# Loading 128 partitions at once, a zero-padded product W, and unsplit float32 output matmuls for one half batch

## The chip, the cores and the metric

The kernel runs on one core of a Trainium2 chip. The metric is the device time of one launch in microseconds (us); a shorter time is better. Three runs of the kernel before gave 950.36, 950.41 and 951.36 us, median 950.41 us.

The core has a matmul engine (PE; its weight loads are the rows of PEld), a vector engine (DVE), an activation engine (ACT), a general engine (POOL) and a sync engine (SP), which here issues nearly all DMAs. Every engine works through its own instructions in order.

## The reference, cut to what matters

Three layers run one after the other. The first is a Nystrom attention over 4 batches, 8 heads, 576 tokens and a head dimension of 64 with 32 landmarks; the second and third are MLPs over the 2304 tokens with 512 features.

```python
q_lm = q.reshape(B, H, 32, 18, D).mean(axis=3)      # k_lm alike
A, Bm, C = sm(q, k_lm), sm(q_lm, k_lm), sm(q_lm, k)
for _ in range(6): Z = 2 * Z - Z @ Bm @ Z
x = (A @ Z @ C @ v)                                 # heads side by side: 2304 x 512
xn = x / sqrt(mean(x * x)) * rms_g
y = silu(xn @ w_gate) * (xn @ w_val) @ w_out        # d_ff 1536
out = (s * relu(y @ w_in2) ** 2 + b) @ w_out2       # d_ff 2048
```

The weights `w_gate`, `w_val`, `w_out`, `w_in2` and `w_out2` arrive as 8-byte floats and are turned into float32 on the chip.

## The kernel before, in words

**Attention and W.** For each batch, A (576 x 32 per head) is kept apart from W = Z C v (32 x 64 per head). The first MLP layer is (A W) w_gate; the kernel computes U = W w_gate first (`fused`), and then multiplies the normalised A with it (`first_mm`). The matrix `gw` holds W transposed and scaled by `rms_g`. One U is built for each of 4 batches x 12 column blocks f of 128 features (48 units, gate and value together). A head has 64 features, so U of one unit takes for each of two groups g four matmuls, one per head, with 64 rows of `gw` and 32 columns (L977).

**Loads.** The 128 partitions of `rawg` are two halves of 64, each with its own heads; the q and k loads (L438) and the loads of `w_gate` and `w_val` (L892) are therefore two DMAs of 64 partitions each. `narrow` loads a 128-column block of 8-byte weights into one of three `stage` buffers, ACT (L902, L904) and DVE (L906, L909) turn it into float32, and `stage` is free again after L906. Batch 0 decodes all blocks of the first MLP and stores the float32 result to DRAM (`keptg`, `kepto`); later batches read it back.

**Split matmuls.** For the big matmuls an operand is split into a high and a low part that the PE takes in one pass each (`split`: L867 or L868 for the high part, L869 for the low part), and three products of such parts stand for one float32 product (`PART3`). `first_mm` (L996), `out_mm` (L1036), `first_mm2` (L960) and `second_mm` (L1062) are such.

**Output matmuls of the first MLP.** A batch is worked on in two halves hf of 288 columns. `hidden` leaves silu(gate) x value of one f and hf in a slot of `hq_r` (a part of `hbuf` and later of `xbuf`); six units later `out_mm` multiplies it with a block of `w_out` (ring `rawo`, three slots) into four PSUM banks.

**Order.** A list scheduler (`Scheduler.run`) writes the order of all engines at build time, from a cost for each operation in microseconds and a key (due time), and it takes ring slots as its own clock says that they come free. Where it has the PE idle in the first 60 us of its clock it puts in small matmuls on ones (L1225) that keep the PE busy. A change of one cost moves instructions on all engines.

**Tail.** From 547 us on the second MLP runs alone (L960 and L1062); no line of it is touched.

Of the kernel before, what the change touches and what calls it, by code (L numbers as in the profile page):

```python
# [222 lines left out]
def t_dve(n):  # L223
    return 0.065 + 0.00104 * n
# [14 lines left out]
def t_mm(n):  # L239
    return 0.0004167 * (max(n, 200) + 32)  # L240
# [7 lines left out]
def tile_nystrom_attention_two_mlps(  # L248
# [39 lines left out]
    def ring(n, shape, name, dtype=F32):  # L288
        return Ring([Slot(sb.tile(shape, dtype, name=f"{name}{i}")) for i in range(n)], True)
# [20 lines left out]
    cm_r = ring(2, [128, 512], "cmag", I32)  # L310
    u_r = [ring(2, [128, 512], f"u{x}", F32R) for x in "hl"]
    w_r = [ring(2, [128, 512], f"w{x}", F32R) for x in "hl"]
    gw_r = ring(2, [128, 128], "gw")
    N_H = 9
    hbuf = sb.tile([128, 1536 + N_H * 288], F32, name="hbuf")
    th_r = Ring([Slot(hbuf[:, 512 * i:512 * i + 512]) for i in range(2)], True)
    h_r = Ring([Slot(hbuf[:, 1024:1536])], True)
# [47 lines left out]
    def consts(_):  # L365
# [10 lines left out]
        out=ident, in_=ones, pattern=[[-1, 128]], compare_op=ALU.is_equal,  # L376
        fill=0.0, base=0, channel_multiplier=1), r=["const"], w=["ident"])

    def load_small(e):
        for i in range(2):  # L380
            e.dma_start(out=gT[D * i:D * i + D], in_=rms_g.rearrange("(r k p) -> r p k", r=2, k=KD)[i])
        e.dma_start(out=s_sb, in_=s2.rearrange("(o k) -> o k", o=1).to_broadcast([128, 1]))
        e.dma_start(out=b_sb, in_=b2.rearrange("(o k) -> o k", o=1).to_broadcast([128, 1]))

# [11 lines left out]
    def attention(b, t0, t1):  # L396
# [38 lines left out]
        for nm, a in (("k", k), ("q", q)):  # L435
            for g in range(2):
                t = src[nm, g] = Buf(qk_r[nm, g])
                at(("sp", 4.1), -0.3 if b else 0, lambda e, t=t, a=a, g=g: [e.dma_start(  # L438
                    out=t.t[64 * i:64 * i + 64].rearrange("p (t d) -> p t d", d=D),
                    in_=a[b, 4 * i + 2 * g:4 * i + 2 * g + 2].rearrange("h (i t) d -> (h i) t d", t=SEG))  # L440
                    for i in range(2)], w=[t])
        vs = Buf(v_r)

        def vt():
            return vs.t.rearrange("p (j h d) -> p j h d", j=5, h=H)
# [213 lines left out]
        def c_side(g, p0):  # L659
# [52 lines left out]
            def cv_mm(_):  # L712
                for j in range(5):
                    n = min(128, S - 128 * j)
                    for h in range(4):
                        nc.tensor.matmul(
                            out=pV.t[32 * h:32 * h + 32, 0:D],
                            lhsT=eT.t[0:n, 128 * j + 32 * h:128 * j + 32 * h + 32],
                            rhs=vt()[0:n, j, 4 * (h // 2) + 2 * g + h % 2, :], start=(j == 0), stop=(j == 4))

            at(("pe", 1.3), p0 + 0.06, cv_mm, r=[(eT, 0), (eT, 1), vs], w=[pV, (Cv, "taken")])
            at({"dve": t_dve(64), "act": 0.1 + t_act(64)}, p0 + 0.07, lambda e: (
# [65 lines left out]
        def wt_mm(_):  # L788
            for g in range(2):
                for h in range(4):  # L790
                    p = slice(32 * h, 32 * h + 32)
                    nc.tensor.matmul(
                        out=pT[h % 2].t[D * (h // 2):D * (h // 2) + D, 32 * g:32 * g + 32],
                        lhsT=Cv.t[p, D * g:D * g + D], rhs=ZY.t[p, 64 * g:64 * g + 32], start=True, stop=True)

        at(("pe", 0.5), 0.62, wt_mm, r=[ZY, (Cv, 0), (Cv, 1)], w=[*pT, (gW, "taken")])
        for i in range(2):
            at(("dve", t_dve(64)), 0.62, lambda e, i=i: e.tensor_tensor(
                out=gW.t.rearrange("p (g c m) -> p g c m", g=2, c=2)[:, :, i],
                in0=pT[i].t[:, 0:64].rearrange("p (g m) -> p g m", g=2),  # L800
                in1=gT.rearrange("p (g c) -> p g c", g=2)[:, :, i:i + 1].to_broadcast([128, 2, 32]),
                op=ALU.mult), r=[pT[i], "small", (gW, "taken")], w=[(gW, i)])

        for hf in range(2):
            p0 = 0.7 + 0.15 * hf
# [64 lines left out]
            out=lo(), in0=src(), in1=hi().bitcast(F32), op=ALU.subtract), r=[*r, wh], w=[wl], pair=True)  # L870
        a.spare = b.spare = {"dve": spare}

    def by_head(x):

        return [x.rearrange("(r k p) f -> r p k f", r=2, k=KD)[i] for i in range(2)]

    def narrow(key, kind, f, part, dst, w, after=()):
        c = slice(128 * f, 128 * f + 128)
        wt = ((w_gate, w_val, w_out), (w_in2, None, w_out2))[kind - 1][part]
        st, a, m = Buf(st_r), Buf(ca_r), Buf(cm_r)  # L880

        def load(e):
            if part == 2:
                e.dma_start(out=st.t, in_=wt[c, :])
            else:
                to = st.t.rearrange("p (k f) -> p k f", k=KD)
                if kind == 2:
                    e.dma_start(out=to, in_=wt[:, c].rearrange("(k p) f -> p k f", p=128))
                    return
                for i in range(2):  # L890
                    p = slice(D * i, D * i + D)
                    e.dma_start(out=to[p], in_=by_head(wt[:, c])[i])  # L892

        def word(i):
            return st.t.bitcast(I32).rearrange("p (n t) -> p n t", t=2)[:, :, i]

        n_ops = len(S_.ops)
        op(("sp", 3.46), key - 12, load, w=[st])
        def low():
            return st.t.bitcast(U8).rearrange("p (n t) -> p n t", t=8)[:, :, 3]  # L900

        op(("act", 0.08 + t_act(512)), key, lambda e: e.activation(  # L902
            out=a.t, in_=word(1).bitcast(F32), func=ACTF.Copy, scale=2.0 ** -112), r=[st, "stage"], w=[a])
# [65 lines left out]
    def fused(key, b, f):  # L969
        r = first_weights(key - 10 if b == 0 else key - 6, b, f)  # L970
        pU, uh, ul = Buf(gv_r), Buf(u_r[0]), Buf(u_r[1])

        def mm(_):
            for g in range(2):
                for h in range(4):
                    k, p = 2 * g + h % 2, slice(D * (h // 2), D * (h // 2) + D)
                    nc.tensor.matmul(  # L977
                        out=pU.t[32 * h:32 * h + 32, 256 * g:256 * g + 256], lhsT=gw[b].t[p, 32 * k:32 * k + 32],
                        rhs=r.t[p, :, 128 * k:128 * k + 128], start=True, stop=True)

        op(("pe", U_PE), key, mm, r=[(gw[b], 0), (gw[b], 1), (r, 0), (r, 1)], w=[pU])
        op({"act": t_act(512), "dve": t_dve(512)}, key, lambda e: (
            e.activation(out=uh.t, in_=pU.t, func=ACTF.Copy) if e is nc.scalar
            else e.tensor_copy(out=uh.t, in_=pU.t)), r=[pU], w=[uh])
        op(("dve", t_dve(512)), key, lambda e: e.tensor_tensor(  # L985
            out=ul.t, in0=pU.t, in1=uh.t.bitcast(F32), op=ALU.subtract), r=[pU, uh], w=[ul])
        return uh, ul
# [35 lines left out]

    def out_mm(key, b, hf, f):
        r = out_weights(key - LEAD_O, b, hf, f)
        w = weights(key - LEAD_O, w_r, lambda: r.t, [r])
        h, hs = hid[b, hf, f], (Buf(hs_r[0]), Buf(hs_r[1]))
        split(key - 2, lambda: hs[0].t[:, 0:HC], lambda: hs[1].t[:, 0:HC], lambda: h.t, [h], *hs, HC)
        h_ops.extend(S_.ops[-2:])
        if f == 0:  # L1030
            acc1[b, hf] = [Buf(acc_r) for _ in range(KD)]
        A = acc1[b, hf]
        for c in range(KD):
            def mm(_, c=c):
                for i, (a, y) in enumerate(PART3):
                    nc.tensor.matmul(  # L1036
                        out=A[c].t[:, 0:HC], lhsT=w[a].t[:, 128 * c:128 * c + 128], rhs=hs[y].t[:, 0:HC],
                        start=(f == 0 and i == 0), stop=(f == F1 - 1 and i == 2))

            op(("pe", 3 * t_mm(HC)), key + 0.4 * c, mm, r=[*w, *hs], w=[A[c]])  # L1040
        if f < F1 - 1:
# [220 lines left out]
```

## Time and profile before

| what | value |
|---|---|
| median of 3 runs | 950.41 us |
| the profiled execution | 949.79 us |
| its span, first to last instruction | 948.1 us |
| PE busy | 894.3 us (94%) |
| DVE busy | 736.9 us (78%) |
| ACT busy | 447.7 us (47%) |
| DMA moved | 105.99 MB |
| mean granted PE clock | 0.986 |

The shares are means over stages that differ. Some 190 us pass before the PE runs without gaps: in this first stage all blocks of the first MLP are loaded and decoded, beside the attention of batches 0 and 1. From there to 547 us the first MLP runs with the attention of the later batches, and then the second MLP.

### The profile page before, as it was taken

To read this page: it belongs to the slowest core of one execution; us is meant where nothing else is said; L and a number is where in the kernel's file an instruction comes from. 1 tells how busy PE (TensorE), PEld (TensorE's weight loads), DVE (VectorE), ACT (ScalarE), POOL (GpSimd) and SP (SyncE) were. 2 spreads that over 40 slices of the span, in tenths; PEclk is the share of its full clock that TensorE was granted. 3 is DMA by queue.
4 is the path that set the end of the run, shared out by engine and by line. 5 is a ranking of instruction groups with operands and counts; after the bars stand their busy time and mean duration, and the time that the engine had idled before them with its cause. 6 is when DMAs were issued, how large, how long until landed. Compare 5 with 4: busy or idle time off the path is not lost.

```text
span 948.1 us, 17201 instructions
## 1 busy us (share of the span) xinstructions
PE 894.3 (94%) x6523; PEld 740.1 (78%) x6523; DVE 736.9 (78%) x1473; ACT 447.7 (47%) x898; POOL 127.9 (13%) x158
## 2 busy tenths in 40 slices
PE   7888988699998999999998999999999999999998
PEld 4566765589877988788887978888888888888886
DVE  6877888998888888879999976676667666666686
ACT  4555465453555344656767333343334333433354
POOL 0460035331363012300000000000000000000000
PEclk9999999799999999999999999999999999999999
DMA  8989878685344432337887200010001000100010
GB/s 174 236 204 274 220 221 243 210 291 160 100 119 131 137 108 84 101 123 246 278 269 241 89 1 1 0 37 9 1 1 45 0 1 1 45 1 0 13 34 22
DMA packets 72787, 105.99 MB, mean 112 GB/s; under 512 B 25856, under 2 KB 46336, under 8 KB 72704
## 3 DMA queue, kind: packets, MB, share of 16 engines
q1 hardware_dynamic: 72512, 104.62, 38.5%
q8 instruction: 51, 0.84, 0.4%
q14 instruction: 32, 0.26, 0.1%
q10 hardware_dynamic: 192, 0.26, 0.1%
HBM read 90.70 MB, written 14.16 MB: 111 GB/s over the span
## 4 chain that ended last, share of the span: by engine, by line
PE 72%; DVE 15%; DMA 6%; issue 4%; ACT 2%; SPq 1%; DVEq 0%; ACTq 0%
PE bank L1062 21%; PE bank L960 20%; PE bank L996 11%; PE bank L1036 10%; PE bank L977 3%; DVE cmag L906 3%; DVE wl L869 2%; DMA stage<-in_moe_w_val_dram 2%; DMA stage<-in_moe_w_out_dram 1%; DMA stage<-in_moe_w_gate_dram 1%; PE bank L1225 1%; PE bank L638 1%; DVE bank L840 1%; DVE hbuf L1013 1%; DVE ul L985 1%
## 5 line engine op out<-in xcount | busy, mean ns | idle before, releaser
L996 PE MATMUL bank<-xh,uh 128*128 128x288 f32 x384 | 124.0, 323 | 17.6 <-DVE ul L985 11.0
L1036 PE MATMUL bank<-hh,wh 128*128 128x288 f32 x384 | 118.8, 309 | 4.9 <-DVE wh L868 3.9
L960 PE MATMUL bank<-xh,uh 128*128 128x512 f32 (+1 forms) x320 | 119.1, 372 | 1.0 <-ACT hbuf L1203 1.0
L960 PE MATMUL bank<-xh,ul 128*128 128x512 f32 (+1 forms) x320 | 118.6, 371 | 0.0
L960 PE MATMUL bank<-xl,uh 128*128 128x512 f32 (+1 forms) x320 | 117.4, 367 | 0.0
L1203 ACT ACTIVATE hbuf<-bank 128x512 f32<-128x512 f32 (+1 forms) x79 | 44.0, 556 | 152.3 <-PE bank L960 152.2
L1036 PE MATMUL bank<-hl,wh 128*128 128x288 f32 x384 | 115.0, 299 | 0.8 <-DVE hl L869 0.7
L1036 PE MATMUL bank<-hh,wl 128*128 128x288 f32 x384 | 114.5, 298 | 0.7 <-DVE wl L869 0.7
L1062 PE MATMUL bank<-wh,hh 128*128 128x512 f32 x288 | 114.3, 397 | 0.3 <-DVE hh L868 0.3
L996 PE MATMUL bank<-xh,ul 128*128 128x288 f32 x384 | 114.4, 298 | 0.0
L996 PE MATMUL bank<-xl,uh 128*128 128x288 f32 x384 | 114.3, 298 | 0.0
L1062 PE MATMUL bank<-wl,hh 128*128 128x512 f32 x288 | 113.8, 395 | 0.0
L1062 PE MATMUL bank<-wh,hl 128*128 128x512 f32 x288 | 113.6, 394 | 0.0
L996 PEld LDWEIGHTS bank<-xh,uh 128*128 128x128 f32 x384 | 72.8, 190 | 43.1 <-DVE ul L985 15.4
L1036 PEld LDWEIGHTS bank<-hh,wh 128*128 128x128 f32 x384 | 73.3, 191 | 11.4 <-DVE wh L868 4.4
L869 DVE TENSOR_TENSOR hl<-hbuf,hh 128x512 fp32r<-128x512 f32 (+2 forms) x137 | 77.4, 565 | 3.0 <-ACT hh L867 0.5
L869 DVE TENSOR_TENSOR wl<-rawo,wh 128x512 fp32r<-128x512 f32 x94 | 70.7, 754 | 5.5 <-ACT wh L867 1.3
L1036 PEld LDWEIGHTS bank<-hl,wh 128*128 128x128 f32 x384 | 73.3, 191 | 2.0 <-DVE hl L869 1.5
L1036 PEld LDWEIGHTS bank<-hh,wl 128*128 128x128 f32 x384 | 73.1, 190 | 1.3 <-DVE wl L869 1.2
L996 PEld LDWEIGHTS bank<-xl,uh 128*128 128x128 f32 x384 | 73.3, 191 | 0.1
L996 PEld LDWEIGHTS bank<-xh,ul 128*128 128x128 f32 x384 | 73.4, 191 | 0.0
L868 DVE CAST uh<-region 128x512 fp32r<-128x512 f32 x57 | 24.3, 427 | 58.8 <-PE bank L960 58.8
(181 smaller groups left out, 1811.4 us busy)
## 6 DMA issues: line engine op xcount, KB each, us to landing
rawo<-kepto SPq DMA_DIRECT2D x84, 256.0 KB, 3.1
rawg<-keptg SPq DMA_DIRECT2D x36, 512.0 KB, 3.9
stage<-in_moe_w_out_dram SPq DMA_DIRECT2D x28, 512.0 KB, 5.0
stage<-in_moe_w_in_dram SPq DMA_DIRECT2D x16, 512.0 KB, 5.4
stage<-in_moe_w_gate_dram SPq DMA_DIRECT2D x24, 256.0 KB, 5.7
stage<-in_moe_w_val_dram SPq DMA_DIRECT2D x24, 256.0 KB, 5.5
keptg<-rawg SPq DMA_DIRECT2D x12, 512.0 KB, 6.9
region<-in_k_dram SPq DMA_DIRECT2D x16, 288.0 KB, 5.6
```

Source lines behind the costliest of these rows:

```text
L638: nc.tensor.matmul(out=ps.t[:, 0:HC], lhsT=part(u, "bd")[:, 128 * e:128 * e + 128], rhs=part(y, "t").rearrange("p (t e i) -> p t e i", e=2 ...
L840: e.reciprocal(out=pS.t[:, 0:HC], in_=pS.t[:, 0:HC])
L868: else e.tensor_copy(out=hi(), in_=src())), r=r, w=[wh], pair=True)
L869: b = op({"dve": t_dve(n), "pool": t_pool(n)}, key, lambda e: e.tensor_tensor(out=lo(), in0=src(), in1=hi().bitcast(F32), op=ALU.subtract) ...
L906: op(("dve", t_dve(512)), key, lambda e: e.scalar_tensor_tensor(out=m.t, in0=word(1), scalar=-2 ** 31, in1=m.t, op0=ALU.bitwise_and, op1=A ...
L960: nc.tensor.matmul(out=ps.t[:, 0:n], lhsT=w[a].t[:, ks], rhs=x[y].t[:, kd, 0:n], start=(kd == 0 and i == 0), stop=(kd == KD - 1 and i == 2))
L977: nc.tensor.matmul(out=pU.t[32 * h:32 * h + 32, 256 * g:256 * g + 256], lhsT=gw[b].t[p, 32 * k:32 * k + 32], rhs=r.t[p, :, 128 * k:128 * k ...
L985: op(("dve", t_dve(512)), key, lambda e: e.tensor_tensor(out=ul.t, in0=pU.t, in1=uh.t.bitcast(F32), op=ALU.subtract), r=[pU, uh], w=[ul])
L996: nc.tensor.matmul(out=ps.t[:, 0:HC], lhsT=u[a].t[:, 256 * g + 128 * part:256 * g + 128 * part + 128], rhs=x[y].t.rearrange("p k n -> p (k ...
L1036: nc.tensor.matmul(out=A[c].t[:, 0:HC], lhsT=w[a].t[:, 128 * c:128 * c + 128], rhs=hs[y].t[:, 0:HC], start=(f == 0 and i == 0), stop=(f == ...
L1062: nc.tensor.matmul(out=A[c].t, lhsT=hs[a].t[:, s], rhs=w[y].t, start=(f == 0 and i == 0), stop=(f == F2 - 1 and i == 2))
L1203: e.activation(out=r.t[:, 0:n], in_=ps.t[:, 0:n], func=ACTF.Relu) if e is nc.scalar
```

## The change

q and k are loaded with four heads in a row on 128 partitions, one DMA instead of two; `w_gate` and `w_val` come as feature = 128 k + partition, one DMA of 512 KB instead of two of 256 KB. A chunk of 128 features holds two heads, so `gw` gets 256 columns instead of 128: for each chunk a block of 128 x 64 with the two heads on its diagonal and zeros elsewhere. POOL writes the zeros once at the start; DVE fills the diagonal in four operations of 64 partitions instead of two of 128. U takes four matmuls of 128 rows and 64 columns instead of eight of 64 rows and 32 columns.

For batch 0, hf 0 (12 of the 96 steps of `out_mm`), one float32 matmul on `rawo` and the hidden slot takes the place of three on split parts, so that no split is made of either. The hidden ring loses one slot (`N_H` 9 to 8).

```diff
-    gw_r = ring(2, [128, 128], "gw")
-    N_H = 9
+    gw_r = ring(2, [128, 256], "gw")
+    N_H = 8
...
+    def gw_zero(e):
+        for s in gw_r.slots:
+            e.memset(s.t, 0.0)
+    op(("pool", 0.6), -30, gw_zero, w=["gw0"])
...
-                at(("sp", 4.1), -0.3 if b else 0, lambda e, t=t, a=a, g=g: [e.dma_start(
-                    out=t.t[64 * i:64 * i + 64].rearrange("p (t d) -> p t d", d=D),
-                    in_=a[b, 4 * i + 2 * g:4 * i + 2 * g + 2].rearrange("h (i t) d -> (h i) t d", t=SEG))
-                    for i in range(2)], w=[t])
+                at(("sp", 3.64), -0.3 if b else 0, lambda e, t=t, a=a, g=g: e.dma_start(
+                    out=t.t.rearrange("p (t d) -> p t d", d=D),
+                    in_=a[b, 4 * g:4 * g + 4].rearrange("h (i t) d -> (h i) t d", t=SEG)), w=[t])
...
-                for i in range(2):
-                    p = slice(D * i, D * i + D)
-                    e.dma_start(out=to[p], in_=by_head(wt[:, c])[i])
+                e.dma_start(out=st.t.rearrange("p (k f) -> p k f", k=KD),
+                            in_=wt[:, c].rearrange("(k p) f -> p k f", p=128))
...
-                        out=pU.t[32 * h:32 * h + 32, 256 * g:256 * g + 256], lhsT=gw[b].t[p, 32 * k:32 * k + 32],
-                        rhs=r.t[p, :, 128 * k:128 * k + 128], start=True, stop=True)
+                        out=pU.t[64 * i:64 * i + 64, 256 * g:256 * g + 256], lhsT=gw[b].t[:, 64 * k:64 * k + 64],
+                        rhs=r.t[:, :, 128 * k:128 * k + 128], start=True, stop=True)
...
+        h, whole = hid[b, hf, f], (b, hf) == (0, 0)
+        if whole:
+            w, hs = [r], [h]
+        else:
+            w = weights(key - LEAD_O, w_r, lambda: r.t, [r])
+            hs = (Buf(hs_r[0]), Buf(hs_r[1]))
+            split(key - 2, lambda: hs[0].t[:, 0:HC], lambda: hs[1].t[:, 0:HC], lambda: h.t, [h], *hs, HC)
...
+                if whole:
+                    nc.tensor.matmul(out=A[c].t[:, 0:HC], lhsT=r.t[:, 128 * c:128 * c + 128], rhs=h.t,
+                                     start=(f == 0), stop=(f == F1 - 1))
+                    return
...
-            op(("pe", 3 * t_mm(HC)), key + 0.4 * c, mm, r=[*w, *hs], w=[A[c]])
+            op(("pe", 0.49 if whole else 3 * t_mm(HC)), key + 0.4 * c, mm, r=[*w, *hs], w=[A[c]])
```

The scheduler writes a new order. On SP, which issues the loads, this stands before after the small loads of the beginning; `in_v` is the v of batch 1 in 18 DMAs, the numbers behind `stage` are its three slots:

```order
L438 DMA region<-in_k_dram 64x1152 x4
L438 DMA region<-in_q_dram 64x1152 x4
L892 DMA stage_90<-in_moe_w_val_dram 64x4x128 x2
L892 DMA stage_91<-in_moe_w_gate_dram 64x4x128 x2
L922 DMA keptg_113<-rawg_84 128x1024
L892 DMA stage_92<-in_moe_w_val_dram 64x4x128 x2
L450 DMA region<-in_v_dram 32x8x64 x18
L892 DMA stage_90<-in_moe_w_gate_dram 64x4x128 x2
```

And in the changed kernel, at the same place on SP:

```order
L443 DMA region<-in_k_dram 128x1152 x2
L443 DMA region<-in_q_dram 128x1152 x2
L454 DMA region<-in_v_dram 32x8x64 x18
L886 DMA stage_90<-in_moe_w_val_dram 128x4x128
L886 DMA stage_91<-in_moe_w_gate_dram 128x4x128
L886 DMA stage_92<-in_moe_w_val_dram 128x4x128
L917 DMA keptg_113<-rawg_84 128x1024
L886 DMA stage_90<-in_moe_w_gate_dram 128x4x128
```

The 18 loads of v have moved ahead of three weight loads (the value block of unit 0 and both blocks of unit 1).

On DVE, around the decode of the second block of `w_out` (`rawo_88`), this stands before:

```order
L906 SCALAR_TENSOR_TENSOR cmag_96<-stage_92,cmag_96 128x512
L909 SCALAR_TENSOR_TENSOR rawo_88<-ca_94,cmag_96 128x512
L868 CAST wh_102<-rawo_88 128x512
L985 TENSOR_TENSOR ul_99<-bank_67,uh_97 128x512
L869 TENSOR_TENSOR wl_104<-rawo_88,wh_102 128x512
L1013 SCALAR_TENSOR_TENSOR hbuf<-hbuf,bank_68 128x288
```

And in the changed kernel:

```order
L901 SCALAR_TENSOR_TENSOR cmag_95<-stage_92,cmag_95 128x512
L904 SCALAR_TENSOR_TENSOR rawo_88<-ca_93,cmag_95 128x512
L980 TENSOR_TENSOR ul_99<-bank_68,uh_97 128x512
L1008 SCALAR_TENSOR_TENSOR hbuf<-hbuf,bank_67 128x288
L625 SCALAR_TENSOR_TENSOR region<-region,bank_69 128x128
L901 SCALAR_TENSOR_TENSOR cmag_96<-stage_90,cmag_96 128x512
```

The two split operations of `rawo_88` are gone, and the next decode follows sooner. Over the whole program DVE has 11 fewer low parts of `w_out` (L869), 7 fewer high parts (L868) and 6 fewer low parts of hidden blocks than before, ACT 14 fewer high parts, POOL 7 fewer low parts.

## Rows read from the trace of the kernel before

**Rows 1.** Windows by stage: stretch, length, engine busy us (instructions), PE clock, DMA share, GB/s.

```profile
50.00:97.00 47.00, 41.58 (x351) 32.54 (x351) 34.97 (x64) 27.43 (x55) 13.89 (x19) 0.93 0.96 248
97.00:190.00 93.00, 73.63 (x731) 56.59 (x730) 81.84 (x175) 49.27 (x107) 26.95 (x32) 0.91 0.78 220
190.00:350.00 160.00, 156.22 (x1482) 137.34 (x1481) 136.97 (x304) 75.24 (x162) 51.33 (x64) 1.00 0.49 152
...
547.00:948.00 401.00, 395.80 (x1800) 325.04 (x1800) 267.79 (x481) 153.16 (x272) 0.00 (x0) 1.00 0.05 13
```

**Rows 2.** Chain of waits, 0 to 190 us: start, length in us, what.

```profile
3.97 7.01 DMA region<-in_q_dram
...
36.03 7.33 DMA stage<-in_moe_w_val_dram
...
67.42 5.18 DMA stage<-in_moe_w_gate_dram
...
76.65 6.95 DMA stage<-in_moe_w_val_dram
...
96.53 6.76 DMA stage<-in_moe_w_gate_dram
...
113.89 0.44 DVE wh L868
114.35 0.69 DVE wl L869
...
177.35 5.47 DMA region<-in_k_dram
...
188.29 0.69 DVE wl L869
```

**Rows 3.** DMA issues on the page: tile, queue, count, KB each, us to landing.

```profile
stage<-in_moe_w_in_dram SPq DMA_DIRECT2D x16, 512.0 KB, 5.4
stage<-in_moe_w_gate_dram SPq DMA_DIRECT2D x24, 256.0 KB, 5.7
```

**Rows 4.** Windows, three short stretches, columns as in rows 1.

```profile
4.00:10.00 6.00, 4.43 (x33) 3.24 (x32) 3.60 (x2) 2.40 (x6) 0.00 (x0) 1.00 1.03 229
62.00:92.00 30.00, 24.86 (x225) 19.71 (x225) 23.39 (x46) 16.36 (x34) 6.36 (x9) 0.94 1.04 274
196.00:208.00 12.00, 12.00 (x107) 10.48 (x106) 11.48 (x21) 6.80 (x14) 6.77 (x9) 1.00 0.97 317
```

**Rows 5.** Timelines of PE (first row) and of the SP queue: start, us, what.

```profile
28.91 0.90 PE L716 MATMUL bank<-region 128*32 128x64 f32 x40
...
42.63 11.96 SPq L450 DMA_DIRECT2D region<-in_v_dram  x18
54.69 1.26 SPq L892 DMA_DIRECT2D stage<-in_moe_w_gate_dram  x2
```

**Rows 6.** Groups by line, 97 to 190 us: busy us, mean ns, idle before.

```profile
L869 DVE TENSOR_TENSOR wl<-rawo,wh 128x512 fp32r<-128x512 f32 x12 | 10.3, 854 | 0.4
...
L868 DVE CAST wh<-rawo 128x512 fp32r<-128x512 f32 x9 | 4.2, 472 | 0.4
...
L869 DVE TENSOR_TENSOR hl<-hbuf,hh 128x288 fp32r<-128x288 f32 x6 | 2.7, 444 | 0.0
```

**Rows 7.** Chain of waits just behind 190 us, columns as in rows 2.

```profile
194.68 1.60 PE bank L1036 x12
196.28 1.00 PE bank L977 x16
```

**Rows 8.** Timeline of PE: two float32 matmuls of 128x128 by 288, back to back.

```profile
41.55 0.65 PE L835 MATMUL bank<-region,ones 128*128 128x288 f32 x2
42.04 0.65 PE L835 MATMUL bank<-xbuf,ones 128*128 128x288 f32 x2
```

**Rows 9.** Windows of 40 ns, line L488 alone: PE and PEld busy (records in flight).

```profile
11.54:11.58 0.04, 0.02 (x2) 0.02 (x2) 1.00 0.84 230
...
11.70:11.74 0.04, 0.04 (x4) 0.04 (x2) 1.00 1.41 346
```

More of the change, by code (lines that the diff above doesn't have):

```diff
@@ L377, in tile_nystrom_attention_two_mlps @@
         fill=0.0, base=0, channel_multiplier=1), r=["const"], w=["ident"])
+    def gw_zero(e):
+        for s in gw_r.slots:
+            e.memset(s.t, 0.0)
+    op(("pool", 0.6), -30, gw_zero, w=["gw0"])
     def load_small(e):
-        for i in range(2):
-            e.dma_start(out=gT[D * i:D * i + D], in_=rms_g.rearrange("(r k p) -> r p k", r=2, k=KD)[i])
+        e.dma_start(out=gT, in_=rms_g.rearrange("(k p) -> p k", p=128))
         e.dma_start(out=s_sb, in_=s2.rearrange("(o k) -> o k", o=1).to_broadcast([128, 1]))
@@ L718, in cv_mm @@
                             lhsT=eT.t[0:n, 128 * j + 32 * h:128 * j + 32 * h + 32],
-                            rhs=vt()[0:n, j, 4 * (h // 2) + 2 * g + h % 2, :], start=(j == 0), stop=(j == 4))
+                            rhs=vt()[0:n, j, 4 * g + h, :], start=(j == 0), stop=(j == 4))
             at(("pe", 1.3), p0 + 0.06, cv_mm, r=[(eT, 0), (eT, 1), vs], w=[pV, (Cv, "taken")])
@@ L792, in wt_mm @@
                     nc.tensor.matmul(
-                        out=pT[h % 2].t[D * (h // 2):D * (h // 2) + D, 32 * g:32 * g + 32],
+                        out=pT[h // 2].t[D * (h % 2):D * (h % 2) + D, 32 * g:32 * g + 32],
                         lhsT=Cv.t[p, D * g:D * g + D], rhs=ZY.t[p, 64 * g:64 * g + 32], start=True, stop=True)
         at(("pe", 0.5), 0.62, wt_mm, r=[ZY, (Cv, 0), (Cv, 1)], w=[*pT, (gW, "taken")])
[L797 to L802, printed above, removed]
+        for i, j in ((0, 0), (0, 1), (1, 0), (1, 1)):
+            at(("dve", t_dve(64)), 0.62, lambda e, i=i, j=j: e.tensor_tensor(
+                out=gW.t.rearrange("p (g c m) -> p g c m", g=2, c=2)[64 * j:64 * j + 64, :, i, 32 * j:32 * j + 32],
+                in0=pT[i].t[64 * j:64 * j + 64, 0:64].rearrange("p (g m) -> p g m", g=2),
+                in1=gT.rearrange("p (g c) -> p g c", g=2)[64 * j:64 * j + 64, :, i:i + 1].to_broadcast([64, 2, 32]),
+                op=ALU.mult), r=[pT[i], "small", "gw0", (gW, "taken")], w=[(gW, i, j)])
         for hf in range(2):
@@ L871, in split @@
         a.spare = b.spare = {"dve": spare}
-    def by_head(x):
-        return [x.rearrange("(r k p) f -> r p k f", r=2, k=KD)[i] for i in range(2)]
     def narrow(key, kind, f, part, dst, w, after=()):
@@ L885, in load @@
             else:
[L886 to L890, printed above, removed]
-                    p = slice(D * i, D * i + D)
-                    e.dma_start(out=to[p], in_=by_head(wt[:, c])[i])
+                e.dma_start(out=st.t.rearrange("p (k f) -> p k f", k=KD),
+                            in_=wt[:, c].rearrange("(k p) f -> p k f", p=128))
         def word(i):
@@ L974, in mm @@
             for g in range(2):
-                for h in range(4):
-                    k, p = 2 * g + h % 2, slice(D * (h // 2), D * (h // 2) + D)
+                for i in range(2):
+                    k = 2 * g + i
                     nc.tensor.matmul(
-                        out=pU.t[32 * h:32 * h + 32, 256 * g:256 * g + 256], lhsT=gw[b].t[p, 32 * k:32 * k + 32],
-                        rhs=r.t[p, :, 128 * k:128 * k + 128], start=True, stop=True)
-        op(("pe", U_PE), key, mm, r=[(gw[b], 0), (gw[b], 1), (r, 0), (r, 1)], w=[pU])
+                        out=pU.t[64 * i:64 * i + 64, 256 * g:256 * g + 256], lhsT=gw[b].t[:, 64 * k:64 * k + 64],
+                        rhs=r.t[:, :, 128 * k:128 * k + 128], start=True, stop=True)
+        op(("pe", U_PE), key, mm, r=[*[(gw[b], i, j) for i in range(2) for j in range(2)], (r, 0), (r, 1)], w=[pU])
         op({"act": t_act(512), "dve": t_dve(512)}, key, lambda e: (
@@ L1025, in out_mm @@
         r = out_weights(key - LEAD_O, b, hf, f)
[L1026 to L1029, printed above, removed]
+        h, whole = hid[b, hf, f], (b, hf) == (0, 0)
[5 more added lines that the diff above has]
+            split(key - 2, lambda: hs[0].t[:, 0:HC], lambda: hs[1].t[:, 0:HC], lambda: h.t, [h], *hs, HC)
+            h_ops.extend(S_.ops[-2:])
         if f == 0:
```

## The prediction

> **What bounds the kernel now.** I read the windows by stage first. In the last 401 us the PE is busy for 395.8 us and the DMA for 5% [rows 1]; nothing of the change stands there. From 190 to 350 us the PE is busy for 156.2 of 160 us, so that stretch is paid by PE work. The slack lies ahead of 190 us: from 97 to 190 us the PE is busy for 73.6 of 93 us at a granted clock of 0.91, DVE for 81.8 us (88%), the DMA for 78%; from 50 to 97 us the DMA for 96% and the PE for 41.6 of 47 us, fillers among them. No engine alone bounds this first stage; the chain of waits says who ends last, and it goes back and forth between landing weights and DVE. The reader is to see there five landings of 64-partition loads behind the attention's first one, at 5.2 to 7.3 us each, and between them the split and decode operations of DVE [rows 2]. So the change is priced in the first 190 us, and what the stage loses in length the total loses, as all behind it follows in order on a PE that is full.
>
> **The loads.** A 64-partition load moves slowly: from 4 to 10 us, when the q and k halves are nearly all there is, the DMA engines are busy all the time (1.03) at 229 GB/s; from 62 to 92 us, where weight halves are mixed with 128-partition stores, at 274/1.04 = 263 GB/s; from 196 to 208 us, with 128-partition transfers alone but a few, at 317/0.97 = 327 GB/s [rows 4]. The changed q, k, gate and value loads have the shape of the last kind; `w_in` has exactly the new shape (512 KB, 1 KB pieces) and lands in 5.4 us, while one half of a gate block, 256 KB, takes 5.7 us [rows 3] and is issued as the second of two that take 1.26 us together [rows 5]. On the chain stand four gate or value landings: 7.33, 5.18, 6.95 and 6.76 us, in all 26.2 us, each with the first half's issue of some 0.63 us ahead of it: 28.7 us. At 5.4 us each they are 21.6 us: 7.1 us less. The k load at 177 us loses one issue of two and about as much landing, 1 us. The opening q landing at 11.0 us comes earlier: 8 loads of 295 KB are 2.36 MB, at 327 instead of 229 GB/s 3.1 us less; DVE's reductions follow it, so I take 1.5 us (ends 0 and 3.1). Sum of the loads 9.6 us; ends 1.5 (issues alone) and 15.
>
> [...]
>
> **The moved v.** The 18 v loads hold SP for 11.96 us, and the next gate load goes out only at 54.69 us [rows 5]. In the new order they stand ahead of three weight loads instead of behind them. The buffer is in use by batch 0 until the matmuls of L716 end, at 29.8 us now [rows 5]; if v starts at 28 to 30 us, the value block of unit 0 goes out near 41 us instead of the 35 to 36 us of now (its landing starts at 36.03 us [rows 2]), while the gate block of unit 2, now held to 54.69 us, is free of the block. Ends: 5 us lost, if unit 0's first matmuls wait for that value block; 6 us won, half the block. I take 0.
>
> **DVE.** Gone are 11 low parts of `w_out` at 0.854 us, 7 high parts at 0.472 and 6 low hidden parts at 0.444 [rows 6]: 9.4 + 3.3 + 2.7 = 15.4 us, all in the 12 steps of batch 0's first half, which lie in this stage. DVE's added operations on `gw` are a few of some 0.2 us per batch, 0.4 us. On the chain I count five low parts between 114.35 and 188.29 us, 4.4 us, five high parts of 0.44 us, 2.2 us, and two hidden parts, 0.7 us (the first and the last stand in [rows 2]): 7.3 us that certainly ended last. ACT and POOL lose work too, but neither is bound here. Ends: 3.5 us, if the next path is close behind, and 15.
>
> **PE.** An unsplit float32 matmul of this shape follows its predecessor after 0.49 us [rows 8]; four make 1.96 us. Now 12 passes take 1.60 us [rows 7]. So each of 12 steps costs 0.36 us more, 4.3 us in all. The PE is idle for 93 - 73.6 = 19.4 us of the second window [rows 1]; I take a quarter on the chain, 1.1 us lost. Ends 0 and 4.3.
>
> **U.** Sixteen records now take 1.00 us [rows 7], four at a time. The new U has 8 records of 128 rows and 64 columns. The landmark matmuls (L488) have just that form, and their records start in pairs: two in flight at 11.54, four at 11.70 us [rows 9]. A record of 256 columns takes 0.49/2 x 256/288 = 0.218 us; four pairs make 0.87 us, about as now. I cost it at 0. Ends: 0.1 us won per unit (48 units, 5 us), or, one after the other, 8 x 0.218 = 1.74 us, 0.74 us lost per unit.
>
> [...]
>
> **Sum.** 9.6 + 0 + 7.3 - 1.1 + 0 = 15.8 us off the chain of the first stage. Three resources are close together there, so other paths will end soon after the one that was cut; I keep three quarters, 11.9 us. 949.79 - 11.9 = 937.9 us for an execution like the profiled one; the median of the runs lies 0.6 us above it: 938.5 us.
>
> **The rivals.**
> - *More: the stage falls to what DVE needs.* From 50 to 190 us DVE is busy for 35.0 + 81.8 = 116.8 us; less 15 it is 101.8. Just behind the stage DVE runs at 11.48/12 = 96% [rows 4]; at that rate the 140 us become 106, floor 916 us. Halfway between the forecast and this floor: 927 us. For it: DVE is at 88% already. Against: the order is fixed at build time and each engine waits in it.
> - *Less: the loads gain nothing but an issue.* If HBM or latency sets the landings, 1.5 + 7.3 - 1.1, three quarters of it, is 5.8 us: 944.6 us.
> - *No change:* the cover is complete, and landings that stay late take back what DVE gives: 949 to 951 us.
> - *Slower: the buffers are held by the PE.* Before, a `rawo` slot and a hidden slot came free when DVE had split them; now only when the PE's fourth matmul has run. With three `rawo` slots the decode of step n + 3 waits for the PE's step n, and DVE works in order: behind a blocked decode queue the low parts of U and the hidden products, for which the PE waits. If each of 9 decodes costs one step's PE time, 9 x 1.96 = 17.6 us are added to the forecast: 956 us. It decides once a decode is blocked for more than 1.3 us on the mean (11.9/9). Against it: a step's three-slot lead is one and a half units.
> - *Slower: U's records run one after the other.* 0.74 us x 36 units behind the first stage, where the PE is full, is 27 us: 965 us. Rows 9 speak against it.
>
> **How the numbers follow.** Forecast 938.5 us: 0.53 (its own range 931 to 945). More, 927: 0.15. Less, 945: 0.13. No change: 0.06. Buffers, 956: 0.10. U, 965: 0.03. A difference of 0.2%, 1.9 us, is about what a measurement can tell from no change. Faster: 0.53 + 0.15 + 0.13 = 0.81. Same 0.06. Slower 0.13. The range from 924 to 951 us leaves out most of the last two cases and the far tail of the second.
>
> **What would show it.** Right: gate and value landings near 5.4 us or less on single issues of 512 KB; the DMA above 290 GB/s when busy between 60 and 95 us; a PE without gaps from some 178 us instead of 190; the tail still 401 us; U's 8 records in about 1 us. Wrong: DVE waits ahead of the `rawo` decodes that PE ends (buffers); U near 1.7 us; landings that stay at 6 to 7 us (less); a stage end at or behind 190 us.

## The result, and the profile after

The changed kernel takes 922.54 us (median of 4 runs, 920.90 to 924.32); the kernel before took 950.38 us beside it (947.47 to 951.36). The ratio is 0.9712 with a 95% interval of [0.9683, 0.9742]: 27.8 us less, where 11.9 were forecast. Four more executions on another chip gave a median of 922.98 us and a ratio of 0.9695 [0.9665, 0.9725]. The direction was right; the time lies just below the range.

The profiled execution took 924.32 us with a span of 922.3. First the windows by stage of the changed kernel, columns as in [rows 1], with the two stretches of [rows 4] that its loads fill, and one of 10 us (147 to 157) in which the PE still loses time:

```profile
4.00:10.00 6.00, 5.68 (x40) 4.32 (x39) 5.37 (x3) 3.61 (x9) 0.00 (x0) 1.00 1.10 347
62.00:92.00 30.00, 25.66 (x208) 19.10 (x206) 25.15 (x51) 19.42 (x44) 5.12 (x6) 1.00 0.82 268
50.00:97.00 47.00, 41.98 (x326) 31.77 (x325) 36.92 (x78) 27.95 (x59) 10.73 (x13) 0.96 0.77 251
97.00:190.00 93.00, 89.07 (x753) 68.49 (x753) 80.94 (x160) 56.46 (x114) 34.76 (x42) 0.96 0.82 269
147.00:157.00 10.00, 6.41 (x35) 5.66 (x34) 9.15 (x16) 9.88 (x15) 1.14 (x2) 0.66 0.72 222
190.00:350.00 160.00, 155.12 (x1432) 135.32 (x1430) 134.04 (x312) 75.66 (x163) 40.57 (x51) 1.00 0.42 127
547.00:922.00 375.00, 370.81 (x1724) 309.96 (x1722) 254.83 (x458) 146.26 (x260) 0.00 (x0) 1.00 0.05 13
```

From 97 to 190 us the PE is now busy for 89.07 of 93 us instead of 73.63, at a clock of 0.96 instead of 0.91 [rows 1]. In the opening the DMA moves 347 GB/s instead of 229, and from 62 to 92 us 268/0.82 = 327 GB/s while busy instead of 263 [rows 4].

The chain of waits of the changed kernel, 0 to 190 us (start, length in us, what), answers to [rows 2]:

```profile
2.20 8.48 DMA region<-in_q_dram
...
41.33 4.89 DMA stage<-in_moe_w_val_dram
...
49.94 4.65 PE bank L1228 x23
...
67.95 5.65 DMA stage<-in_moe_w_val_dram
...
79.22 6.43 DMA stage<-in_moe_w_gate_dram
...
133.75 4.17 DMA stage<-in_moe_w_val_dram
...
149.99 0.61 DVE ul L980
150.65 1.81 PE bank L991 x6
...
158.92 1.01 PE bank L972 x8
...
160.92 1.94 PE bank L1035 x8
```

The gate and value landings are still there, but shorter: the four take 4.89 + 5.65 + 6.43 + 4.17 = 21.1 us together. The five low parts of `w_out` are gone, and from 150.65 us the chain runs on the PE alone. Eight U records (L972) take 1.01 us, as sixteen took 1.00 [rows 7]; eight records of the unsplit matmuls (L1035, in pairs) take 1.94 us. The page's DMA issues (tile, queue, count, KB each, us to landing), as in [rows 3]:

```profile
stage<-in_moe_w_gate_dram SPq DMA_DIRECT2D x12, 512.0 KB, 4.9
stage<-in_moe_w_val_dram SPq DMA_DIRECT2D x12, 512.0 KB, 5.4
```

A whole gate block lands in 4.9 us, less time than the 5.7 us of a half [rows 3]. The SP queue (start, us, what), as in the last of [rows 5]:

```profile
24.73 16.49 SPq L454 DMA_DIRECT2D region<-in_v_dram  x18
41.33 0.39 SPq L886 DMA_DIRECT2D stage<-in_moe_w_val_dram  x1
41.83 0.44 SPq L886 DMA_DIRECT2D stage<-in_moe_w_gate_dram  x1
```

The moved v now holds the queue for 16.49 us instead of 11.96, and unit 0's value block goes out behind it, at 41.33 us. The groups of DVE from 97 to 190 us, as in [rows 6]:

```profile
L873 DVE TENSOR_TENSOR wl<-rawo,wh 128x512 fp32r<-128x512 f32 x5 | 3.8, 756 | 0.7 <-ACT wh L871 0.5
L873 DVE TENSOR_TENSOR hl<-hbuf,hh 128x288 fp32r<-128x288 f32 x2 | 0.9, 454 | 0.0
```

What is left of them belongs to the second half. To see where the 25.5 us between the two profiled executions lie, the table takes the start of the first U record of units 8, 12 and 47 and the end of the last matmul, all read from the instructions of each profiled execution. From about unit 12 on, the output matmuls are those of batch 0's second half; the last column is the stretch from unit 47 to the end, in which nothing was meant to change. The kernels below "after" are described in the next section.

| kernel (short) | median us | ratio to before | unit 8 | unit 12 | unit 47 | end | 47 to end |
|---|---|---|---|---|---|---|---|
| before | 950.38 | 1 | 117.6 | 187.7 | 506.8 | 943.8 | 437.0 |
| after | 922.54 | 0.9712 [0.9683, 0.9742] | 116.6 | 167.1 | 489.4 | 918.1 | 428.7 |
| halves again | 935.53 | 0.9829 [0.9810, 0.9849] | 126.1 | 179.4 | 500.5 | 930.1 | 429.7 |
| all split | 939.78 | 0.9874 [0.9819, 0.9929] | 115.3 | 184.6 | 506.7 | 935.8 | 429.1 |
| unsplit alone | 935.99 | 0.9830 [0.9802, 0.9858] | 117.3 | 170.7 | 489.2 | 926.1 | 436.9 |
| splits kept, unread | 933.74 | 0.9801 [0.9771, 0.9831] | 118.9 | 177.7 | 499.9 | 929.4 | 429.5 |
| both halves unsplit | 927.60 | 0.9734 [0.9705, 0.9762] | 116.1 | 169.4 | 494.9 | 926.4 | 431.6 |
| v in its old place | 919.90 | 0.9665 [0.9638, 0.9692] | 112.1 | 162.7 | 482.6 | 911.1 | 428.5 |

After against before: 1.0 us is won by unit 8, 20.6 by unit 12, 17.3 are left at unit 47, and the last stretch adds 8.3.

Each of these starts is read from one profiled execution. Kernels of the next section that keep the order and the loads of another kernel show how far they scatter: unit 12 starts at 166.6 to 168.3 us in five executions in the order of after, at 160.5 to 163.6 in six with v in its old place, and at 187.7 and 191.5 in the two in the order of before. So two kernels that differ by less than some 3 us there are not told apart by one profile each.

### The profile page after: what moved, and what is told of

The parts are those of the page before. It is cut to its first block, busy times and chain, and to the rows that moved or that the text cites. A ratio compares the mean times of both kernels' runs of the same rounds, so it can differ in the third digit from the quotient of the medians.

```text
span 922.3 us, 16186 instructions
## 1 busy us (share of the span) xinstructions
PE 881.8 (96%) x6077; PEld 734.5 (80%) x6077; DVE 722.4 (78%) x1454; ACT 444.9 (48%) x885; POOL 124.1 (13%) x154
## 3 DMA queue, kind: packets, MB, share of 16 engines
q1 hardware_dynamic: 71856, 104.62, 36.2%
## 4 chain that ended last, share of the span: by engine, by line
PE 76%; DVE 11%; DMA 5%; issue 3%; ACT 3%; SPq 0%; DVEq 0%; ACTq 0%
PE bank L1065 21%; PE bank L955 21%; PE bank L991 13%; PE bank L1039 10%; PE bank L972 3%; DVE cmag L901 2%; DMA stage<-in_moe_w_val_dram 2%; PE bank L1035 2%; DMA stage<-in_moe_w_out_dram 1%; PE bank L642 1%; PE bank L1228 1%; PE bank L580 1%; DVE wl L873 1%; DMA region<-in_q_dram 1%; DVE rawg L904 1%
## 5 line engine op out<-in xcount | busy, mean ns | idle before, releaser
L991 PE MATMUL bank<-xh,uh 128*128 128x288 f32 x384 | 127.1, 331 | 14.6 <-DVE ul L980 12.9
L955 PE MATMUL bank<-xl,uh 128*128 128x512 f32 (+1 forms) x320 | 117.6, 368 | 0.0
L955 PE MATMUL bank<-xh,ul 128*128 128x512 f32 (+1 forms) x320 | 117.6, 368 | 0.0
L1065 PE MATMUL bank<-wh,hh 128*128 128x512 f32 x288 | 112.4, 390 | 0.3 <-DVE hh L872 0.3
L991 PEld LDWEIGHTS bank<-xh,uh 128*128 128x128 f32 x384 | 73.3, 191 | 40.1 <-DVE ul L980 16.8
L1039 PE MATMUL bank<-hh,wh 128*128 128x288 f32 x336 | 101.1, 301 | 0.0
L1039 PE MATMUL bank<-hl,wh 128*128 128x288 f32 x336 | 99.6, 296 | 1.0 <-DVE hl L873 1.0
L1039 PE MATMUL bank<-hh,wl 128*128 128x288 f32 x336 | 99.0, 295 | 0.0
L873 DVE TENSOR_TENSOR hl<-hbuf,hh 128x512 fp32r<-128x512 f32 (+2 forms) x126 | 73.6, 585 | 2.4
L991 PEld LDWEIGHTS bank<-xl,uh 128*128 128x128 f32 x384 | 73.7, 192 | 0.7
L991 PEld LDWEIGHTS bank<-xh,ul 128*128 128x128 f32 x384 | 73.5, 191 | 0.0
L955 PEld LDWEIGHTS bank<-xh,uh 128*128 128x128 f32 x320 | 60.2, 188 | 12.6 <-ACT hbuf L1206 1.2
L955 PEld LDWEIGHTS bank<-xl,uh 128*128 128x128 f32 x320 | 60.0, 188 | 11.0
L955 PEld LDWEIGHTS bank<-xh,ul 128*128 128x128 f32 x320 | 60.1, 188 | 10.0
L1039 PEld LDWEIGHTS bank<-hh,wh 128*128 128x128 f32 x336 | 63.2, 188 | 3.6 <-issue 2.1
```

The costliest lines, as they stand in the source:

```text
L873: b = op({"dve": t_dve(n), "pool": t_pool(n)}, key, lambda e: e.tensor_tensor(out=lo(), in0=src(), in1=hi().bitcast(F32), op=ALU.subtract) ...
L955: nc.tensor.matmul(out=ps.t[:, 0:n], lhsT=w[a].t[:, ks], rhs=x[y].t[:, kd, 0:n], start=(kd == 0 and i == 0), stop=(kd == KD - 1 and i == 2))
L991: nc.tensor.matmul(out=ps.t[:, 0:HC], lhsT=u[a].t[:, 256 * g + 128 * part:256 * g + 128 * part + 128], rhs=x[y].t.rearrange("p k n -> p (k ...
L1039: nc.tensor.matmul(out=A[c].t[:, 0:HC], lhsT=w[a].t[:, 128 * c:128 * c + 128], rhs=hs[y].t[:, 0:HC], start=(f == 0 and i == 0), stop=(f == ...
L1065: nc.tensor.matmul(out=A[c].t, lhsT=hs[a].t[:, s], rhs=w[y].t, start=(f == 0 and i == 0), stop=(f == F2 - 1 and i == 2))
```

## The experiments

**The loads as halves, all else as after.** The q, k, gate and value loads are two DMAs of 64 partitions each; the order of the instructions is that of after.

```diff
...
-                e.dma_start(out=st.t.rearrange("p (k f) -> p k f", k=KD),
-                            in_=wt[:, c].rearrange("(k p) f -> p k f", p=128))
...
+                for i in range(2):
+                    p = slice(64 * i, 64 * i + 64)
+                    e.dma_start(out=st.t.rearrange("p (k f) -> p k f", k=KD)[p],
+                                in_=wt[:, c].rearrange("(k p) f -> p k f", p=128)[p])
```

> The changed kernel in the same order on every engine, but each load of q, k, w_gate and w_val is issued as two DMAs of 64 partitions again. If the faster landing of 128-partition loads made the gain (theory loads): 8 us or more slower than the changed kernel, 930 us or later, and the DMA's rate while busy in the first 100 us back near 230 to 260 GB/s. If DVE's missing splits made it (theory DVE): at most 3 us slower, 922 to 926 us.

935.53 us. All of it is lost by unit 8 to 12 (126.1 and 179.4 instead of 116.6 and 167.1), so in the new order the 128-partition loads are worth some 12 us. In the opening the halves move 224 GB/s where the whole loads of after, in the same order, move 347 (columns as in [rows 1]):

```profile
4.00:10.00 6.00, 3.39 (x22) 2.39 (x21) 3.28 (x2) 1.53 (x4) 0.00 (x0) 0.81 1.02 224
```

The queue shows where the delay goes: the 18 v loads stand from 34.18 to 48.33 us, and unit 0's value block goes out at 48.44.

```profile
34.18 14.15 SPq L455 DMA_DIRECT2D region<-in_v_dram  x18
48.44 1.32 SPq L893 DMA_DIRECT2D stage<-in_moe_w_val_dram  x2
```

**All output matmuls split, the loads and W as after.**

```diff
-        h, whole = hid[b, hf, f], (b, hf) == (0, 0)
+        h, whole = hid[b, hf, f], False
```

> The changed kernel with the output matmuls of batch 0's first half on split operands as before (the scheduler orders anew). Theory DVE: the units 8 to 12, where 20 us were won, take about 70 us again instead of 50, total 938 to 943 us. Theory loads: the unsplit matmuls were worth little, total 922 to 930 us.

939.78 us. Unit 8 starts as early as in after, and then units 8 to 12 take 69.3 us again (before: 70.1; after: 50.5). So the gain of this stretch comes from the unsplit matmuls. Loads and W alone win 3.1 us by unit 12, about as much as the starts scatter. Its windows show what the PE has in these units; columns as in [rows 1]:

```profile
97.00:190.00 93.00, 76.38 (x662) 59.33 (x661) 81.23 (x170) 49.60 (x106) 29.64 (x34) 0.82 0.71 221
...
127.00:137.00 10.00, 10.00 (x73) 6.52 (x65) 6.60 (x18) 1.29 (x3) 5.77 (x9) 0.50 0.62 145
157.00:167.00 10.00, 5.55 (x24) 5.21 (x24) 9.32 (x13) 3.82 (x7) 0.00 (x0) 0.52 0.57 189
```

From 157 to 167 us DVE is busy for 9.32 of 10 us while the PE has work for 5.55, at a granted clock of 0.52. From 127 to 137 us the PE is busy all the time, but at a clock of 0.50. The kernel before shows the like in a window of its own, at a clock of 0.66:

```profile
167.00:177.00 10.00, 6.40 (x34) 4.34 (x34) 9.76 (x16) 6.35 (x13) 3.88 (x4) 0.66 0.51 189
```

**The unsplit matmuls alone, on the kernel before.**

```diff
-        w = weights(key - LEAD_O, w_r, lambda: r.t, [r])
-        h, hs = hid[b, hf, f], (Buf(hs_r[0]), Buf(hs_r[1]))
...
+        h, whole = hid[b, hf, f], (b, hf) == (0, 0)
+        if whole:
+            w, hs = [r], [h]
...
```

> The kernel before with the unsplit output matmuls of batch 0's first half alone (64-partition loads, old W, nine hidden slots; the scheduler orders anew). Theory DVE: units 8 to 12 gain some 15 to 20 us, total 930 to 935 us, with the tail as slow as before. Theory loads: 942 to 950 us.

935.99 us. By unit 12 it wins 17.0 us with the old loads (by the medians of whole executions the unsplit matmuls are worth 15.6 us here, 951.55 - 935.99, and 17.2 between all split and after); the two halves of the change add up (17.0 + 3.6 = 20.6, or 3.1 + 17.5). But its last stretch is as long as that of before, 436.9 us, while all split has the short one, 429.1: that part of the gain belongs to neither the matmuls nor the loads.

**The last stretch: where buffers lie.** The change makes `gw` 1024 bytes larger per partition and `hbuf` 1152 smaller, so the split hidden buffers `hh` and `hl`, which the last stage uses too, and the region behind them move down by 128 bytes. Modulo 512, `hh` starts at 320 instead of 448. Four kernels move them with a tile that nobody uses, the first and the fourth on after, the second on before, the third on after with the tile behind `hh` and `hl`, so that only the region goes back; the order is that of their base, and the diff is that of the fourth.

```diff
+    sb.tile([128, 32], F32, name="pad")
     hs_r = [ring(2, [128, 512], nm, F32R) for nm in ("hh", "hl")]
+    sb.tile([128, 224], F32, name="pad2")
...
```

All back to the addresses of before:

> The changed kernel with an unused tile of 128 bytes per partition ahead of the split hidden buffers, so that these and the big region lie where they lay before; the order is the same. If the place of these buffers made the 7 us of the untouched second MLP: the distance of its matmuls goes from 227 back to 230 and 233 ns, total 928 to 930 us. If the chip or the run made it: 922 us, 227 ns.

The kernel before with 896 bytes of padding, `hh` at 320:

> The kernel before with an unused tile of 896 bytes per partition ahead of the split hidden buffers, so that these and the big region lie at the same place modulo 1024 bytes as in the changed kernel; order unchanged. If the place alone made the tail's 7 us: matmuls 226 to 227 ns apart instead of 231, 942 to 945 us. If the gain needs something else of the change: 950 us, 231 ns.

After, the region alone moved back:

> The changed kernel with the 128 bytes behind the split hidden buffers: only the big region (second MLP's weights, read by DVE and ACT) lies where it lay before, the hidden buffers (read by PE) lie as in the changed kernel. If PE's own reads of the hidden buffers set the 231 ns: 226 to 227 ns and 922 to 925 us. If the region's place does it: 231 ns and 928 to 930 us.

After, `hh` and `hl` alone moved back:

> After with 128 unused bytes per partition ahead of the split hidden blocks (hh, hl) and 896 behind them: only hh and hl stand where they stand in the kernel before, the region of weights and x does not (it moves by 1024). If the PE's reads of hh and hl make the slow tail, 231.4 ns per matmul and about 929 us; if it is the distance of some other pair of buffers, 226 ns and about 923 us.

| kernel | median us | `hh` modulo 512 | ns per matmul, 570 to 870 us |
|---|---|---|---|
| after, all moved back | 930.06 | 448 | 231.4 |
| before, padded | 944.97 | 320 | 226.7 |
| after, region moved back | 924.61 | 320 | 225.7 |
| after, `hh`, `hl` moved back | 929.69 | 448 | 231.4 |

Before itself has 231.4, after 226.4. The kernel before, padded, is faster than unpadded by a ratio of 0.9929 [0.9903, 0.9955] with no other edit. Moving the region alone changes nothing that can be told (924.61 us, beside 922.98 for after). So the address of `hh` and `hl` alone is worth about 7 us. The profile gives no wait for it; the PE is busy throughout in both and only does more. The window of before from 600 to 850 us, columns as in [rows 1]:

```profile
600.00:850.00 250.00, 250.00 (x1083) 203.19 (x1082) 164.03 (x288) 92.35 (x154) 0.00 (x0) 1.00 0.05 13
```

and that of after:

```profile
600.00:850.00 250.00, 250.00 (x1105) 207.08 (x1104) 167.52 (x293) 94.26 (x157) 0.00 (x0) 1.00 0.05 13
```

**The splits kept as work that nobody reads.** After, with the 12 steps' split operations still done; the matmuls stay unsplit.

```diff
         if whole:
+            weights(key - LEAD_O, w_r, lambda: r.t, [r])
+            dead = (Buf(hs_r[0]), Buf(hs_r[1]))
+            split(key - 2, lambda: dead[0].t[:, 0:HC], lambda: dead[1].t[:, 0:HC], lambda: h.t, [h], *dead, HC)
             w, hs = [r], [h]
```

> After, with the split operations of the first half's w_out and hidden blocks kept as work whose results nobody reads; the matmuls stay unsplit. If the gain of units 8 to 12 is the work of DVE and ACT that fell away, it comes back: unit 12 starts near 184 us and the time is about 938 to 940 us. If the gain is that PE no longer waits for the splits, unit 12 starts near 168 us and the time is about 923 us.

933.74 us: between the two. Unit 12 starts at 177.7 us, 10.6 later than in after and 6.9 earlier than in all split. Over the whole program DVE is busy for 738.5 us, as in all split (741.3); after has 722.4. Its window:

```profile
97.00:190.00 93.00, 78.85 (x667) 57.40 (x667) 84.07 (x173) 55.59 (x119) 29.54 (x33) 0.91 0.73 230
```

So by this run about three fifths of the gain is work that DVE and ACT no longer do (10.6 of 17.5 us), and about two fifths that the PE no longer waits for the split results. The clock from 97 to 190 us differs too (0.82 in all split, 0.91 here, 0.96 in after), and its part in either share was not separated. Both theories hold in part. The shares are rough: each start scatters by up to 3 us, and since nobody waits for the unread splits, the scheduler may put them where they cost less than in all split.

**Both halves of batch 0 unsplit.**

```diff
-        h, whole = hid[b, hf, f], (b, hf) == (0, 0)
+        h, whole = hid[b, hf, f], b == 0
```

> After, with the output matmuls of batch 0's second half unsplit as well. That half lies behind unit 12, where PE is full: if the unsplit form costs PE 0.36 us a step, 12 steps, 4 us more than after, about 927 us. If DVE or ACT bounds there too, it is faster than after, 918 us or less.

927.60 us. From unit 12 to 24 it takes 121.5 us where after takes 117.2: 4.3 us more, and 12 x 0.36 are 4.3. So where the PE is full (here busy for 96.56 of 100 us from 190 to 290 us), the 0.36 us a step seem to be paid in whole. The close agreement may be chance: in this execution, the slowest of its five, the granted clock from 190 to 290 us is 0.97 (after: 1.00); the medians differ by 5.1 us.

**v in its old place.** After, with batch 1's v load ordered behind three weight loads again.

```diff
         at(("sp", 9.5), -0.25 if b else 0.01, load_v, w=[vs])
+        if b == 1:
+            mine[-1].after = 30.0
```

> The changed kernel with the v loads of batch 1 held back in the scheduler until 30 us of its clock, so that on SP they stand behind the same three weight loads and the store as in the kernel before. If the moved v ate what the loads give in the first 60 us (unit 1 starts at 59.0 us in both kernels though unit 0 is 3.9 us earlier): unit 1 near 54 us, total 917 to 920 us. If the attention's own chain holds unit 1: unit 1 at 58 to 59 us, total 921 to 925 us.

919.90 us, a little faster than after: on the same chip its four executions took 917.37 to 921.00 us and those of after 921.35 to 926.18. (The intervals to before, [0.9638, 0.9692] and [0.9683, 0.9742], overlap by a hair.) Unit 12 starts 4.4 us earlier. Its SP queue:

```profile
31.89 0.38 SPq L888 DMA_DIRECT2D stage<-in_moe_w_val_dram  x1
33.89 0.38 SPq L888 DMA_DIRECT2D stage<-in_moe_w_gate_dram  x1
36.80 0.37 SPq L888 DMA_DIRECT2D stage<-in_moe_w_val_dram  x1
37.22 1.41 SPq L919 DMA_DIRECT2D keptg<-rawg  x1
38.72 9.99 SPq L454 DMA_DIRECT2D region<-in_v_dram  x18
```

Unit 0's value block goes out 9.4 us earlier, and v holds the queue for 9.99 us instead of 16.49. Unit 0 itself starts no earlier (41.2 us; after 41.7); units 1 and 2 do (55.8 and 63.9; after 59.0 and 66.5).

**Which addresses are slow.** Five more kernels put `hh` and `hl` of this last version at other addresses, by an unused tile of 64 to 256 bytes ahead of them; the one at 64 was timed in three rounds, the others have one execution each.

> The version with v held back to its old place in SP's queue, and 256 unused bytes ahead of hh and hl, so that they stand at 64 instead of 320 modulo 512. If only the old place (448) is slow, the cadence stays at 224 to 226 ns and the time at 919 to 920 us; if each place has its own cadence, it differs from both by a few ns, 4 us per 2 ns and more.

> The version with v held back to its old place in SP's queue, with hh and hl at 384 modulo 512. In the tail a slice of 128 columns of hh or hl (512 bytes) is loaded as weights. If an address that is a multiple of 128 bytes and below the slow 448 is fast, 226 to 227 ns per matmul between 600 and 850 us and a last stage of 428 to 430 us; if slowness grows toward 512, 228 to 231 ns.

> The same with hh and hl at 416 modulo 512, which is no multiple of 64. If the boundary lies between 384 and 416 (a row of 288 columns then reaches into a fourth stretch of 512 bytes), 231 ns and a last stage of 436 us; if only 448 itself is slow, 227 ns.

> The same with hh and hl at 480 modulo 512. By a boundary between 384 and 416, 231 ns and 436 us; if only 448 is slow, 227 ns.

> The same with hh and hl at 0 modulo 512, so that no slice of 512 bytes crosses a multiple of 512. If crossing costs something, this is the fastest, under 226 ns and a last stage under 428 us; else 226 to 227 ns.

| `hh` modulo 512 | time, us | unit 47 to the end | matmul records, 600 to 850 us |
|---|---|---|---|
| 0 | 920.32 | 430.3 | 1099 |
| 64 | 919.25 (median) | 429.5 | 1105 |
| 320 (no tile) | 919.90 (median) | 428.5 | 1105 |
| 384 | 926.57 | 436.1 | 1084 |
| 416 | 928.38 | 436.3 | 1085 |
| 480 | 925.25 | 436.8 | 1080 |

384 is slow too. With 448 from the runs above, four places from 384 to 480 are slow and three from 0 to 320 are not; between 64 and 320 nothing was tried. A whole multiple of 512 brings nothing extra. Two things stay open. The remainder of 512 is a way to name the places, and that the pattern repeats is not shown: all slow starts of `hh` lie between 160128 and 160224 bytes, the fast ones at 160064, 160256, 160320 and, in the kernel before with padding, 161088. And the other operands of these matmuls (`xh`, `xl`, `uh`, `ul`, `wh`, `wl`) start at 320 modulo 512 in every kernel, so no run tells the place of `hh` and `hl` from their distance to those. The two fastest versions, `hh` at 320 and at 64, cannot be told apart.

## Why the prediction was wrong in size

Three steps failed: the quarter that was taken off the sum, the DVE term, and the tail that was put at nothing. All three made the forecast gain too small; the term for loads and v was too large and offset a part of that.

**"I keep three quarters".** The sum was 15.8 us and 11.9 were kept, because other paths were taken to end soon behind the one that was cut. Unit 12 starts 20.6 us earlier: nothing was lost on the way, and 4.8 more than the sum were won. These 4.8 are the difference of two larger errors: the unsplit matmuls gave 17.0 us where 7.3 - 1.1 = 6.2 were counted, loads and moved v 3.6 where 9.6 were. That the sum still came within 5 us of the start of unit 12 is luck.

**DVE.** 7.3 us were counted for operations that certainly ended last. The unsplit matmuls are worth 17.0 us by unit 12 (unsplit alone), above the upper end of 15. The chain counts an operation only where it ended last. DVE was busy 88% of the time and works in order, so a removed operation can bring the next decode forward too; that fits the 10.6 us that splits kept unread cost, but the single steps were not traced. The other 6.9 us are a term the sum lacked, by the same run: the PE's own wait for split results fell away (before, L1036 waits from 97 to 190 us 3.9 us for `wh` and 0.7 for `wl`). Part of both may be the clock: 0.91 in 97 to 190 us before, 0.82 in all split, 0.96 after. How much of the gain the clock makes alone was not separated.

**Loads and moved v.** With "unsplit alone" and "v in its old place" as the ends, four kernels give the start of unit 12 by form of load and place of v (unsplit alone has the old W, whose U takes as long):

| unit 12 starts, us | v in its old place | v moved ahead |
|---|---|---|
| loads in halves | 170.7 | 179.4 |
| loads of 128 partitions | 162.7 | 167.1 |

The loads are worth 8.0 us with v in its old place and 12.3 with it moved (the 170.7 is from the fastest of its four executions, 3.9 us under their median, so the 8.0 may be too small). The 9.6 lies between them, and the four landings on the chain took 21.1 us where 21.6 were forecast; but the opening's 1.5 us did not come through the q landing, which is 0.3 us earlier (10.68 against 10.98). The moved v was put at 0 with 5 us lost at the worst: it loses 4.4, nearly that end. The place for the value block, near 41 us, was right (41.33), but by luck: v went out at 24.73 us instead of 28 to 30, and held the queue for 16.49 us instead of 11.96. Together loads and v are worth 3.6 us net, and 9.6 stood in the sum.

In the opening halves move 229 GB/s in the kernel before [rows 4] and 224 in the order of after, whole loads 347. The rival of loads that gain nothing but an issue is not borne out: by unit 12 halves cost 12.3 us (179.4 against 167.1). What sets these rates was not shown: a half differs from a whole load both in its partitions and in the number of DMAs, and no run here separates the two.

**PE and U.** The unsplit form was worked out to take 1.96 us a step, 0.36 more than the 1.60 of the split one [rows 7]; its eight records take 1.94 us. In the first half that cost was not seen, and the second half shows some 4.3 us. U is right: 1.01 us against 1.00, no term. The PE ran without gaps from 150.65 us (busy for all of the 39.35 us to 190), not from 178.

**The tail: "nothing of the change stands there".** Wrong, by 8.3 us. No instruction of that stage was changed, but some of its operands lie elsewhere, and nine kernels with moved buffers show the two levels. No rival named it. With all buffers moved back the changed kernel takes 930.06 us, inside the range that was forecast; without this miss the time would have stayed in it.

**Given back, in this execution.** Of the 20.6 us at unit 12, 17.3 are left at unit 47. Most of the 3.3 stands in units 40 to 44, where the attention is over and `w_in2` is already decoded. Before and after, from 430 to 466 us:

```profile
430.00:466.00 36.00, 35.21 (x298) 31.00 (x298) 33.62 (x67) 22.84 (x46) 1.79 (x1) 1.00 0.82 268
```

```profile
430.00:466.00 36.00, 31.56 (x217) 27.93 (x215) 31.39 (x60) 24.05 (x48) 1.90 (x2) 0.95 0.85 282
```

After, the PE waits for DVE (the split low part of U, 3.8 us in three waits) and the clock falls to 0.95; units 40 to 44 take 36.2 us instead of 33.0. But after with the region moved back, in the same order, has the clock at 1.00 there and takes 33.1 us:

```profile
430.00:466.00 36.00, 32.86 (x240) 28.98 (x237) 33.65 (x65) 25.65 (x52) 1.92 (x2) 1.00 0.88 293
```

The kernel before, padded, takes 35.1. So the 3.3 us are within what executions of one order differ by, and are not shown to belong to the change.

**The account.** 937.9 us were forecast for the profiled execution and 924.3 measured: 8.3 us in the tail, 4.8 above the sum, 3.9 for the quarter that was not lost, less 3.3 given back, make 13.7 of the 13.6 missed. The rival of a stage that falls to what DVE needs (927 us) came closest in number, in part by luck, since 8.3 us came from the tail, of which it knew nothing. Its reason holds in part: work of DVE and ACT made 10.6 of the 17.5 us.

## What to carry to other kernels

Where an engine that works in order is nearly full (DVE 88%), a removed operation can be worth more than its share of the chain: here splits that kept DVE busy for 16.1 us (738.5 against 722.4) cost 10.6, and the chain had counted 7.3. Add what the other engines no longer wait for, and take a share off only for a path that you can name. A load order that frees one queue entry can fill the queue ahead of a more urgent one, as v did here for 16.49 us ahead of unit 0's value block: ask what the block waits for at its new place. And an edit that changes a buffer's size moves all buffers behind it, here by 128 bytes, with some 7 us in the tail: compare addresses before calling a stage untouched. Last, profile one order more than once before explaining a few microseconds between two profiles.

## What the runs showed of the hardware that had not been expected

In these runs the time of the last stage, where the PE is busy for 250.00 of 250 us, differs with where the split hidden buffers start: 226.2 to 227.5 ns per matmul record (250 us over 1105 to 1099 records, 600 to 850 us) with `hh` and `hl` at 0, 64 or 320 modulo 512 bytes, 230.4 to 231.5 (1085 to 1080 records) at 384, 416, 448 or 480, at the same clock (1.00) and with matmuls of the same form; 436 to 437 against 428 to 432 us from unit 47 to the end. From 570 to 870 us a weight load takes 188 to 189 ns on the mean in before and in after, and five of the six groups of matmuls, two that do not read `hh` or `hl` among them, look longer in the profile (393 to 396 ns before, the sixth 388; 388 to 389 after); the mechanism is open.
